# A new order for the attention and the first MLP of a fused attention and two-MLP kernel

## The chip, the cores and the metric

One core of one Trainium2 chip runs the kernel in one launch. The metric is the device time of that core in microseconds (us). Smaller is better.

## The reference

The inputs are q, k and v of shape (2, 8, 768, 64), that is two sequences with eight heads, and the weights of two MLPs. All of it is float32.

```python
# attention, per head: keys in a window of 16 to either side, and one summary key for each block of 32
k_sum = k.reshape(B, H, nb, 32, D).max(axis=3)
v_sum = v.reshape(B, H, nb, 32, D).mean(axis=3)
scores_l = where(|i - j| < 16, scale * q @ k.T, -1e9)
scores_s = scale * q @ k_sum.T + log(32)
a = softmax(concatenate([scores_l, scores_s]))
x = a @ concatenate([v, v_sum])            # (1536 tokens, 512)
# first MLP, 512 -> 2048 -> 512
h = x @ w_in;  x = (h * sigmoid(h)) @ w_out
# second MLP, 512 -> 1536 -> 512
out = ((x @ w_a) * (x @ w_b)) @ w_out2
```

## The kernel before

Every large product is made of three matmuls of parts: each float32 operand is split into a rounded high part and the rest (the low part), and high by high, high by low and low by high are added up in one PSUM bank. The weights come in as 64-bit words of which a float32 is put together on the chip.

The attention runs in 24 steps of 64 queries with all eight heads. Steps 0 to 11 belong to the first sequence. The MLPs work on blocks of 512 tokens, each of which needs eight steps, so the first MLP's work on one block stands between the attention's steps for later ones. TensorE (PE) takes its instructions in the order written, and so do VectorE (DVE), ScalarE (ACT), GpSimd (POOL) and the DMA queue on SyncE (SP).

That order, for everything up to the end of the attention, is a table of words in one string, ORDER. A loop calls one function for each word. The last letter of many words names the engine: a for ACT, v for DVE, p for POOL. The words that matter here:

- Attention step n: `sc:n` scores on PE, `sm:n` mask and row maxima on DVE, `ex:n` the exponential on ACT, `rs:n` sums and their reciprocal on DVE, `no:n` the multiplication by it, `tr:n` transposition on PE, `pc:n` copy of that out of PSUM, `av:n` the product with the values on PE, `xh:n` and `xl:n` its high and low part. `tq` and `tk` are transpositions of q and k on PE, `mk` block maxima of k on DVE.
- Value means of the first sequence: `sv:0:g` sums for head pair g on POOL or DVE, `mv:0:g` the matmuls behind them.
- Weight tile f of w_in or w_out: `da:in:f` and `du:in:f` take the two halves of the words apart (ACT, L468, and DVE, L474), `dj:in:f` joins them (DVE, L478), `hi:in:f` makes the high part (L146 on ACT, L148 on DVE), `lo:in:f` the low part (L501 on POOL or DVE). `hR` and `lR` do the last two again for a w_out tile that was put aside in DRAM.
- MLP tile i, which is block i // 16 and weight tile i % 16: `m1:i` 12 matmuls into h, `sg:i` SiLU, `gh:i` and `gl:i` high and low part of the result, `m2:i` 12 matmuls that add to y.

A softmax step has two forms. Steps in the set ACTS subtract the maximum and add up within ACT's exponential (four instructions, L393). The others subtract on POOL (`su:n`, L387), take one exponential (L396) and sum on DVE (L401).

PSUM has eight banks. Two belong to h. Four are added to the attention's two until the word `boot`, and are y's from then on. So after `boot` every `sc`, `tr`, `av`, `tq`, `tk` and `mv` takes the next of two banks in turn, here called a0 and a1, and `sc` takes both:

```python
ps = [bank(f"sc{n}")[:, 0:2 * KK].rearrange("p (a c) -> p a c", a=2) for _ in range(2)]
```

The next user of a bank waits until the one before has been read: scores by `sm`, a transposition by `pc`, an `av` by `xl`.

Of the kernel before, what the change touches and what calls it, by code (L numbers as in the profile page):

```python
# [29 lines left out]
wk:0:2:1 bq:0:1:1:v LG:0:2 sc:1 sm:1 pk:0:2:a LG:0:0 LI:1 LG:0:3 pk:0:1:v sc:0 sm:0 ex:1 sc:2 LI:0 sv:0:0:4:p LQ:0:2  # L30
sc:5 sm:2 LV:0 sm:5 ex:0 LV:1 sv:0:3:4:v rs:1 ex:2 sv:0:2:1:p mv:0:0:512:4 no:1:p ex:5 rs:0 du:in:1 mv:0:1:0:1
mv:0:2:0:1 mv:0:3:0:4 tr:1 sc:3 no:0:p rs:2 no:2:p tq:0:2:0 du:in:0 tr:0 sm:3 kv:0:0:a pc:1:a sc:4 sm:4 tq:0:2:1 su:4:p
tr:2 PV:0:1 pc:0:v rs:5 ex:3 bq:0:2:0:a sc:7 av:0 LV:2 rs:3 sm:7 ex:4 av:1 no:3:p su:7:p bq:0:2:1:a PV:0:2 LV:3 rs:4
pc:2:v da:in:1 tr:3 sc:6 no:5:p xh:0:a xh:1:a sm:6 xl:0 PV:0:3 LI:3 av:2 ex:7 tr:5 xl:1 rs:7 no:4:p pc:3:a sc:8 no:7:p
sm:8 LV:4 ex:6 LV:5 LV:6 av:3 LV:7 rs:6 xh:2:a xh:3:a no:6:p pc:5:a LI:4 tr:4 pc:4:a da:in:0 xl:2 sc:9 ex:8 dj:in:1 xl:3
sm:9 LI:2 hi:in:1:v av:5 tr:6 sc:11 lo:in:1:p av:4 xh:5:a pc:6:a tr:7 sm:11 pc:7:a rs:8 xl:5 sc:10 av:6 xh:4:a LV:8
LQ:1:0 av:7 da:in:4 m1:1:0 su:11:p ok:1 no:8:p dj:in:0 xh:6:a du:in:4 xl:4 xh:7:a xl:7 hi:in:0:a LK:1:1 lo:in:0:p xl:6
tr:8 ex:11 dj:in:4 m1:1:1 m1:0:0 ex:9 rs:11 sm:10 pc:8:a rs:9 hi:in:4:v m1:0:1 sg:1:p LO:0 da:in:3 no:9:p da:in:2
tq:1:0:0 av:8 tk:1:1:0 du:in:3 tr:9 lo:in:4:p LK:1:2 gh:1:a LI:6 du:in:2 LO:1 gl:1:p sg:0:v dj:in:2 LO:2 no:11:p
bq:1:0:0:a gh:0:a dj:in:3 du:out:0 hi:in:2:a xh:8:v tq:1:0:1 tk:1:1:1 lo:in:2:p hi:in:3:a gl:0:v da:out:0 m1:4 dj:out:0  # L40
bq:1:0:1:a sg:4:p xl:8 du:in:6 mk:1:1:0 lo:in:3:p gh:4:a du:out:1 tr:11 pc:11:a m1:2:0 pc:9:a da:in:6 da:out:1 LI:8
hi:out:0:v m1:2:1 tk:1:2:1 mk:1:2:1 dj:out:1 dj:in:6 mk:1:1:1 wk:1:1:0 LI:5 wk:1:2:1 du:in:8 SP:0 boot gl:4:p du:out:2
tk:1:2:0 hi:out:1:a hi:in:6:a sg:2:p wk:1:2:0 lo:out:0:p m1:3 da:out:2 lo:out:1:p lo:in:6:p m2:0 dj:out:2 wk:1:1:1
gh:2:a gl:2:p du:in:5 LK:1:0 da:in:5 m2:1 LO:3 SP:2 hi:out:2:v sg:3:p dj:in:5 tk:1:0:0 m1:6 LO:4 hi:in:5:a LG:1:1
mk:1:2:0 du:out:3 lo:out:2:p da:out:3 tk:1:0:1 gh:3:a LI:7 sg:6:p mk:1:0:0 mk:1:0:1 lo:in:5:p SP:1 dj:out:3 m2:2 LO:6
sk:1:v da:in:8 LO:5 hi:out:3:a du:out:4 da:out:4 SP:3 gl:3:p dj:in:8 wk:1:0:0 hi:in:8:a lo:out:3:p dj:out:4 wk:1:0:1
lo:in:8:p da:out:6 LI:10 du:out:6 pk:1:0:v LI:9 m1:5 da:in:7 du:in:7 gh:6:a m2:3 sg:5:v gl:6:p dj:out:6 dj:in:7 LV:11
du:out:5 sc:13 LO:8 hi:out:4:a hi:in:7:a gh:5:a lo:out:4:p sm:13 sc:14 gl:5:v SP:4 lo:in:7:p m1:8 hi:out:6:a da:in:9
du:in:9 m1:7 sg:8:v da:out:5 dj:in:9 sm:14 LV:9 dj:out:5 sc:12 LO:7 hi:in:9:v lo:out:6:p du:in:10 ex:10 rs:10 LG:1:2
lo:in:9:p LV:10 SP:6 m2:4 hi:out:5:a sm:12 da:in:10 lo:out:5:v sg:7:p av:9 dj:in:10 xh:9:a LI:13 no:10:p da:out:7 SP:5  # L50
ex:14 du:out:7 m2:5 m2:6 LQ:1:1 du:out:8 xl:9 LI:11 sv:1:2:1:p gh:8:a ex:13 da:out:8 hi:in:10:v dj:out:7 gh:7:a
lo:in:10:p hi:out:7:a tr:10 ex:12 gl:7:p gl:8:v SP:7 da:in:13 du:in:13 LG:1:3 sv:1:3:1:p dj:out:8 LO:9 lo:out:7:v LG:1:0
du:in:11 m1:9 LI:12 mv:1:2:256:1 sv:1:1:1:p da:in:11 dj:in:13 m1:10 pc:10:a LO:13 hi:out:8:a rs:14 du:out:9 rs:13
dj:in:11 lo:out:8:v du:in:12 av:10 sg:9:p sg:10:p mv:1:3:0:1 kv:1:2:a m2:7 SP:8 hi:in:11:a xh:10:a LI:15 hi:in:13:v
# [5 lines left out]
dj:out:11 da:in:14 PV:1:2 PV:1:3 sm:16 av:12 xh:12:a LV:14 lo:out:10:p du:in:14 gh:13:a hi:out:11:v xl:12 SP:11 m2:10  # L60
rs:15 SP:10 no:15:p da:out:13 dj:in:14 sg:12:v dj:out:13 PV:1:1 tr:13 pc:13:a sc:17 LO:15 lo:out:11:v hi:in:14:a
da:out:12 gh:12:a hi:out:13:a lo:out:13:p LO:14 lo:in:14:p sm:17 av:14 xh:14:a SP:13 gl:12:v m2:11 tr:15 xl:14 m1:15
gl:13:p da:out:15 sg:15:p du:out:12 LQ:1:2 dj:out:12 pc:15:v SP:12 du:out:14 av:15 hi:out:12:a av:13 xh:15:v da:out:14
lo:out:12:p ex:18 LV:17 m1:14 xh:13:a RO:16 xl:15 du:out:15 gh:15:v LV:16 ex:16 m2:12 hR:16:v xl:13 gl:15:p sg:14:p
dj:out:14 lR:16:v dj:out:15 m1:17 sc:19 sg:17:v ex:17 hi:out:14:a gh:17:v gl:17:v m2:13 gh:14:a sm:19 tq:1:2:0
lo:out:14:p rs:18 m1:16 hi:out:15:a tq:1:2:1 lo:out:15:v rs:17 RO:17 gl:14:p no:17:v sg:16:v bq:1:2:0:v no:18:p
bq:1:2:1:a m1:18 tr:17 m2:14 SP:15 rs:16 sg:18:v LV:18 pc:17:v sc:20 sm:20 su:19:p av:17 RO:19 first gh:16:a m2:15
gl:16:v ex:19 xh:17:v rs:19 su:20:p yh:0:1 xl:17 hR:17:a SP:14 no:19:p hR:19:v LV:21 no:16:v tr:18 m1:21 RO:18 pc:18:a
sc:22 yh:0:0 lR:17:p sm:22 yh:0:3 tr:16 yh:0:2 sg:21:p gh:18:v gl:18:v pc:16:v lR:19:v sc:21 m1:19 m2:16 gh:21:v gl:21:p
RO:20 ex:20 sg:19:p RO:23 hR:18:v sm:21 av:18 xh:18:v xl:18 m2:17 lR:18:p tr:19 ex:22 gh:19:v hR:20:a pc:19:v ex:21  # L70
av:16 gl:19:p rs:20 m1:24 m1:20 LV:19 sg:24:p m2:18 rs:22 xh:16:a rs:21 xl:16 sc:23 sg:20:v no:21:p RO:21 lR:20:v
hR:23:a sm:23 tr:21 av:19 m2:19 gh:20:a LV:20 gl:20:v LV:22 no:22:p RO:22 pc:21:a gh:24:v ex:23 m1:22 sg:22:p av:21
hR:21:a rs:23 m2:20 hR:22:a xh:19:v xl:19 gl:24:p lR:21:p RO:27 gh:22:v m1:27 LV:23 lR:23:v sg:27:p no:20:v gl:22:p
m2:21 m1:23 sg:23:p tr:22 no:23:p xh:21:v xl:21 lR:22:p tr:23 pc:23:a gh:27:v RO:25 gl:27:p hR:27:v m2:22 RO:24 pc:22:v
# [1015 lines left out]
```

## Time and profile before

| what | value |
|---|---|
| time, median of 3 runs | 640.61 us (639.71 to 643.76) |
| the profiled execution | 643.56 us, of which its span is 641.8 us |
| mean granted TensorE clock | 0.989 of full speed |
| busy: PE, DVE, ACT, POOL | 612.9, 396.1, 299.7, 303.9 us |

The span runs from the first to the last instruction. The profiled execution lies 2.95 us above the median of the runs. The attention and its share of the first MLP take the first 250 us of the span, and the words of ORDER end there.

### The profile page before, as it was taken

The page shows a single profiled execution, that of the slowest core. Times are in us where ns is not written, and L with a number is a line of the kernel's source. Part 1 is how long each engine was busy: PE and PEld are TensorE (multiplying, and loading weights), DVE is VectorE, ACT ScalarE, POOL GpSimd, SP SyncE. Part 2 cuts the span into 40 slices and gives each one's busy share as a digit, 9 for nine tenths or more (in the row PEclk, how much of TensorE's full clock was granted, in tenths as well). Part 3 has the DMA queues.
Part 4 walks back from the last instruction along what each step waited for, and adds up shares of the span by engine and source line. Part 5 has one row for each costly group of instructions (what it writes and reads, how often), then busy time and mean ns, then how long its engine had stood idle before and what let it go on. Part 6 is the DMA issues. An engine that isn't in the chain of part 4 may idle for free.

```text
span 641.8 us, 10139 instructions
## 1 busy us (share of the span) xinstructions
PE 612.9 (95%) x3632; PEld 528.8 (82%) x3632; DVE 396.1 (62%) x768; ACT 299.7 (47%) x651; POOL 303.9 (47%) x270
## 2 busy tenths in 40 slices
...
GB/s 231 204 177 258 283 249 308 154 203 103 62 46 58 59 37 146 229 221 195 165 199 189 116 49 73 191 104 225 83 213 83 229 16 97 84 182 302 142 2 132
DMA packets 90522, 97.82 MB, mean 152 GB/s; under 512 B 39000, under 2 KB 68440, under 8 KB 90472
## 3 DMA queue, kind: packets, MB, share of 16 engines
...
q8 instruction: 29, 0.48, 0.3%
q14 instruction: 21, 0.17, 0.1%
...
## 4 chain that ended last, share of the span: by engine, by line
PE 71%; DVE 4%; POOL 4%; issue 2%; ACT 0%; ACTq 0%; DVEq 0%; POOLq 0%
PE y L557 17%; PE h L524 15%; PE bankg L762 10%; PE bankh L762 10%; PE ol L808 10%; PE o L787 5%; POOL wab L645 1%; POOL ab L727 1%; PE av L428 1%; POOL w_out L501 1%; PE sc L358 1%; PE pt L414 1%; DVE yt L677 1%; DVE pts L148 0%; DVE sm L380 0%
## 5 line engine op out<-in xcount | busy, mean ns | idle before, releaser
L524 PE MATMUL h<-x,w_in 128*128 128x512 f32 (+1 forms) x612 | 143.0, 384 | 0.0
L557 PE MATMUL y<-g,w_out 128*128 128x512 f32 x576 | 141.3, 396 | 0.0
L524 PEld LDWEIGHTS h<-x,w_in 128*128 128x128 f32 x612 | 109.9, 190 | 22.3 <-issue 0.5
L557 PEld LDWEIGHTS y<-g,w_out 128*128 128x128 f32 x576 | 107.5, 189 | 23.9 <-issue 0.5
L501 POOL TENSOR_TENSOR w_out<-re_out,w_out 128x512 fp32r<-128x512 f32 x37 | 52.4, 1416 | 114.2 <-ACT w_out L146 108.0
L808 PE MATMUL ol<-w_out,plh 128*128 128x512 f32 x192 | 59.1, 389 | 0.0
L539 DVE TENSOR_TENSOR g<-h,g 128x512 fp32r<-128x512 f32 x31 | 21.4, 691 | 46.7 <-ACT g L146 46.5
L501 POOL TENSOR_TENSOR w_out<-w_out,w_out 128x512 fp32r<-128x512 f32 x23 | 32.0, 1402 | 34.1 <-ACT w_out L146 29.5
L539 POOL TENSOR_TENSOR g<-sg,g 128x512 fp32r<-128x512 f32 x17 | 24.8, 1461 | 43.7 <-DVE g L148 18.8
L727 POOL TENSOR_TENSOR ab<-sum,ab 128x384 f32<-128x384 f32 x24 | 27.9, 1171 | 32.2 <-DVE sum L724 32.1
L532 ACT ACTIVATE h<-h 128x512 f32<-128x512 f32 x31 | 18.1, 583 | 53.8 <-PE h L524 53.7
L808 PEld LDWEIGHTS ol<-w_out,plh 128*128 128x128 f32 x192 | 36.0, 188 | 7.5
L146 ACT CAST w_out<-re_out 128x512 fp32r<-128x512 f32 x38 | 23.6, 622 | 36.4 <-issue 27.5
L808 PE MATMUL ol<-w_out,pll 128*128 128x512 f32 x96 | 37.4, 389 | 0.0
L800 DVE TENSOR_TENSOR pll<-pl,plh 128x1024 fp32r<-128x1024 f32 x12 | 17.9, 1492 | 29.9 <-ACT plh L799 29.9
L787 PE MATMUL o<-w_out,p 128*128 128x512 f32 x108 | 30.7, 397 | 0.4 <-POOL w_out L501 0.2
L380 DVE CUSTOM_DVE_ANT_0 sm<-sc,mask 128x120 f32<-128x120 f32 x96 | 21.1, 276 | 15.5 <-PE sc L358 15.4
L393 ACT ACTIVATE sm<-sm,st 128x120 f32<-128x120 f32 x76 | 29.1, 390 | 1.5 <-DVE st L380 1.4
L478 DVE SCALAR_TENSOR_TENSOR w_out<-w_out,u_out 128x512 uint32<-128x512 uint32 x28 | 27.3, 974 | 3.0 <-ACT w_out L468 1.5
L762 PE MATMUL bankh<-yhT,wab 128*128 128x384 f32 x96 | 28.3, 335 | 0.7 <-DVE sum L709 0.7
L408 POOL TENSOR_TENSOR sm<-sm,st 128x480 f32<-128x480 f32 x20 | 22.6, 1136 | 11.7 <-DVE st L404 5.3
L501 POOL TENSOR_TENSOR w_in<-w_in,w_in 128x512 fp32r<-128x512 f32 x15 | 21.3, 1424 | 13.5 <-ACT w_in L146 7.9
(260 smaller groups left out, 1377.8 us busy)
## 6 DMA issues: line engine op xcount, KB each, us to landing
...
```

Of the source, the lines that this page charges most:

```text
L146: nc.scalar.copy(o, i)
L393: nc.scalar.activation(sm[:, pr, :], sm[:, pr, :], AF.Exp, scale=-1.0, bias=st[:, 0, pr:pr + 1], accum_out=st[:, 1, pr:pr + 1])
L408: engines[engine].tensor_tensor(sm, sm, st[:, 3, :, None].to_broadcast([P, NPR, KK]), op=ALU.mult)
L478: nc.vector.scalar_tensor_tensor(bits, bits, 3, u_t.pop((kind, f)), op0=ALU.logical_shift_left, op1=ALU.bitwise_or)
L501: engine.tensor_tensor(w[:, 1], w32_t[kind, f], w[:, 0].bitcast(F32), op=ALU.subtract)
L524: nc.tensor.matmul(h_ps[i][:, cols], win_t[f][:, a, c * P:(c + 1) * P], x_t[n][:, steps, m, c, :], start=(idx == 0), stop=(idx == 3 * NK - 1))
L539: engines[engine].tensor_tensor(g_t[i][:, 1], sg_t.pop(i), g_t[i][:, 0].bitcast(F32), op=ALU.subtract)
L557: nc.tensor.matmul(y_ps[n, c], wout_t[i][:, a, c * P:(c + 1) * P], g_t[i][:, m, :], start=(f == 0 and (a, m) == (0, 0)), stop=(f == N1 - 1 ...
L727: engines["v" if k == 6 else "p"].tensor_tensor(at, x, at, op=ALU.mult)
L762: nc.tensor.matmul((A, B)[b], weights(u, a, s, s + 1)[:, 0, c * P:(c + 1) * P], yc_t[q, y][m][:, c, :], start=(idx == 0 and not more), sto ...
L787: nc.tensor.matmul(o_ps[t], g[:, a, c:c + P], w[:, m], start=(begins and (a, m) == (0, 0)), stop=(ends and (a, m) == PARTS[-1]))
L808: nc.tensor.matmul(late_o[j], late_p[f][a][:, j * P:(j + 1) * P], wo2_t[N2 + f][:, m], start=(f == 0 and (a, m) == (0, 0)), stop=(f == N2 ...
```

## The change

ORDER is replaced by another order of almost the same words, and ACTS by another set. No function is changed. Steps 7, 11 and 19 join ACTS, and 10 and 23 leave it, so one subtraction fewer stands on POOL. Of the words that stay, these change their engine:

- from POOL to DVE: 11 `lo` (in 3, 4, 6, 8, 10, 11 and out 0, 2, 9, 10, 12), 9 `no` (0, 4, 8, 9, 12, 14, 18, 19, 21), 3 `lR` and 6 `gl`; from DVE to POOL: one `no`, 3 `lR`, 2 `gl` and one copy of block maxima;
- between ACT and DVE: copies and high parts (`br`, `pc`, `xh`, `hi`, `hR`, `gh`), in either direction; on balance DVE loses one `hi`, two `hR`, one `gh` and two `xh` to ACT and takes one `pc`.

```diff
-ACTS = {0, 1, 2, 3, 5, 6, 8, 9, 10, 12, 13, 14, 15, 16, 17, 18, 21, 22, 23}
+ACTS = {0, 1, 2, 3, 5, 6, 7, 8, 9, 11, 12, 13, 14, 15, 16, 17, 18, 19, 21, 22}
...
-pc:14:v m1:13 sc:18 ex:15 pk:1:2:a m2:9 du:out:10 LO:11 SP:9 no:13:v gh:11:v da:out:10 hi:in:12:a lo:in:12:p LV:13
...
+m1:12 da:out:11 pc:12:v lo:in:15:v du:out:11 sg:13:p LV:13 gh:13:a sc:16 dj:out:11 PV:1:2 hi:out:10:a da:in:14 sm:16
```

PE in the first sequence, where the value means are made (`vsum00` is the tile of the means, `vg00` to `vg03` are the four head pairs' sums, `pt1` is the transposition `tr:1`). Before:

```order
L358 MATMUL sc5_327<-kin0_169,qbm_204 64x120
L312 MATMUL vsum00_362<-vg00_283,sel_89 120x128 x4
L312 MATMUL vsum00_362<-vg01_249,sel_89 120x128
L312 MATMUL vsum00_362<-vg02_264,sel_89 120x128
L312 MATMUL vsum00_362<-vg03_287,sel_89 120x128 x4
L414 MATMUL pt1_382<-ident_87,sm1_276 120x128 x4
```

And now:

```order
L358 MATMUL sc5_326<-kin0_153,qbm_210 64x120
L312 MATMUL vsum00_358<-vg00_280,sel_89 120x128 x4
L312 MATMUL vsum00_358<-vg03_287,sel_89 120x128 x4
L312 MATMUL vsum00_358<-vg01_204,sel_89 120x128
L312 MATMUL vsum00_358<-vg02_268,sel_89 120x128
L414 MATMUL pt1_380<-ident_87,sm1_282 120x128 x4
```

The four matmuls for head pair 3, whose sums DVE makes, moved ahead of those for pairs 1 and 2, whose sums POOL makes.

DVE early in the first MLP, around the low part of the first w_out tile (`w_out0`; u tiles are `du`, w32 tiles `dj`, `ks1` is `mk`, `pts11` is `pc:11`). Before:

```order
L474 TENSOR_SCALAR u_out1_920<-st_out1_861 128x512
L148 CAST w_out0_951<-w32_out0_893 128x512
L274 TENSOR_REDUCE ks1_736<-kt121_965 128x4x8
L478 SCALAR_TENSOR_TENSOR w32_out1_946<-w32_out1_946,u_out1_920 128x512
L478 SCALAR_TENSOR_TENSOR w32_in6_944<-w32_in6_944,u_in6_914 128x512
L274 TENSOR_REDUCE ks1_736<-kt111_884 128x4x8
L474 TENSOR_SCALAR u_in8_982<-st_in8_949 128x512
L474 TENSOR_SCALAR u_out2_990<-st_out2_866 128x512
```

And now:

```order
L478 SCALAR_TENSOR_TENSOR w32_out0_908<-w32_out0_908,u_out0_871 128x512
L148 COPY pts11_928<-pt11_919 120x512
L501 TENSOR_TENSOR w_in3_905<-w32_in3_828,w_in3_905 128x512
L474 TENSOR_SCALAR u_out1_933<-st_out1_860 128x512
L274 TENSOR_REDUCE ks1_746<-kt121_954 128x4x8
L478 SCALAR_TENSOR_TENSOR w32_out1_951<-w32_out1_951,u_out1_933 128x512
L274 TENSOR_REDUCE ks1_746<-kt111_883 128x4x8
L539 TENSOR_TENSOR g4_926<-sg4_911,g4_926 128x512
L478 SCALAR_TENSOR_TENSOR w32_in6_935<-w32_in6_935,u_in6_913 128x512
L474 TENSOR_SCALAR u_in8_1007<-st_in8_917 128x512
L474 TENSOR_SCALAR u_out2_1009<-st_out2_867 128x512
L501 TENSOR_TENSOR w_out0_959<-w32_out0_908,w_out0_959 128x512
```

The low parts of `w_in3` and `w_out0` and the copy `pts11` came to DVE (the low parts from POOL), the high part of `w_out0` left it for ACT, and the low part of `w_out0` stands behind `u_out2`.

PE in the second sequence, around the transposition `pt12` (`tr:12`) and the scores `sc16`, whose two tiles are the two banks (y rows are `m2`, h rows are `m1`). Before:

```order
L414 MATMUL pt12_1719<-ident_87,sm12_1334 120x128 x4
L358 MATMUL sc16_1732<-kout1_735,qb_90 64x120
L358 MATMUL sc16_1733<-kout1_735,qb_90 64x120
...
L524 MATMUL h12_1742<-x0_522,w_in12_1703 128x512 x12
L428 MATMUL av12_1769<-pts12_1730,vw0_91 64x64 x8
L557 MATMUL y0_0_1025<-g10_1563,w_out10_1757 128x512 x3
...
L414 MATMUL pt13_1812<-ident_87,sm13_1230 120x128 x4
L358 MATMUL sc17_1819<-kin1_734,qb_90 64x120
...
L428 MATMUL av14_1850<-pts14_1649,vw2_93 64x64 x8
```

And now:

```order
L414 MATMUL pt12_1716<-ident_87,sm12_1319 120x128 x4
L524 MATMUL h12_1723<-x0_527,w_in12_1702 128x512 x12
L358 MATMUL sc16_1749<-kout1_745,qb_90 64x120
L358 MATMUL sc16_1750<-kout1_745,qb_90 64x120
...
L428 MATMUL av12_1772<-pts12_1739,vw0_91 64x64 x8
L414 MATMUL pt13_1790<-ident_87,sm13_1233 120x128 x4
L557 MATMUL y0_0_1030<-g10_1565,w_out10_1761 128x512 x3
...
L428 MATMUL av14_1832<-pts14_1644,vw2_93 64x64 x8
L414 MATMUL pt15_1850<-ident_87,sm15_1554 120x128 x4
```

The MLP tile `h12` moved between `pt12` and `sc16`, and `av12` and `pt13` now stand directly behind `sc16`. `sc17` went further down, to where it follows a whole tile of y.

## Rows read from the trace of the kernel before

**Rows 1.** Windows: stretch, length; busy us (instructions) of PE, PEld, DVE, ACT, POOL; clock, DMA, GB/s.

```profile
40.00:60.00 20.00, 19.39 (x239) 17.55 (x240) 19.76 (x52) 17.31 (x44) 14.15 (x14) 1.00 0.95 268
60.00:80.00 20.00, 20.00 (x103) 16.90 (x102) 18.41 (x25) 14.79 (x36) 13.13 (x11) 1.00 0.88 260
0.00:250.00 250.00, 226.17 (x1712) 182.45 (x1713) 159.46 (x447) 154.59 (x376) 114.22 (x112) 0.97 0.59 161
```

**Rows 2.** Timeline of PE from the value means to the first transposition.

```profile
19.64 1.35 PE L312 MATMUL vsum<-vg,sel 96*120 96x128 f32 x10 [1.48 <-POOL vg L298]
...
22.60 2.49 PE L312 MATMUL vsum<-vg,sel 96*120 96x128 f32 x10 [1.61 <-POOL vg L298]
...
24.88 1.06 PE L414 MATMUL pt<-ident,sm 128*120 128x128 f32 x4
```

**Rows 3.** Timeline of PE after `boot`: start, length, what; idle time before it and its releaser.

```profile
84.90 1.04 PE L358 MATMUL sc<-kin,qb 64*64 64x120 f32 x16 [2.05 <-DVE st L380]
...
132.02 0.63 PE L358 MATMUL sc<-kout,qb 64*64 64x120 f32 x14 [0.83 <-DVE pts L148]
...
140.28 0.63 PE L358 MATMUL sc<-kin,qb 64*64 64x120 f32 x14 [0.33 <-ACT pts L146]
141.55 0.69 PE L428 MATMUL av<-pts,vw 120*64 120x64 f32 x16 [0.64 <-PE sc L358]
...
172.16 0.69 PE L428 MATMUL av<-pts,vw 120*64 120x64 f32 x16 [0.65 <-PE sc L358]
...
180.35 0.62 PE L414 MATMUL pt<-ident,sm 128*120 128x128 f32 x4 [0.80 <-DVE st L380]
...
182.59 0.86 PE L358 MATMUL sc<-kin,qb 64*64 64x120 f32 x14 [1.27 <-DVE pts L148]
...
206.26 0.63 PE L414 MATMUL pt<-ident,sm 128*120 128x128 f32 x4 [0.69 <-DVE st L380]
```

**Rows 4.** Timeline of POOL: the low part of the first w_out tile.

```profile
62.14 1.30 POOL L501 TENSOR_TENSOR w_out<-w_out,w_out 128x512 fp32r<-128x512 f32 x1 [0.69 <-DVE w_out L148]
```

**Rows 5.** Timeline of PE at the first tiles of y.

```profile
64.84 5.61 PE L557 MATMUL y<-g,w_out 128*128 128x512 f32 x24
```

**Rows 6.** Windows around two stretches of low granted clock, columns as in Rows 1.

```profile
19.00:22.40 3.40, 1.35 (x10) 1.16 (x10) 1.79 (x13) 3.40 (x21) 3.24 (x4) 1.00 1.14 271
22.50:29.20 6.70, 6.60 (x46) 5.62 (x50) 2.54 (x15) 3.30 (x13) 3.38 (x4) 0.50 0.83 148
179.40:182.80 3.40, 1.33 (x22) 0.81 (x17) 3.06 (x12) 3.34 (x5) 0.00 (x0) 1.00 0.00 0
182.90:186.20 3.30, 3.30 (x21) 2.42 (x11) 0.23 (x1) 0.54 (x1) 0.00 (x0) 0.50 0.60 139
```

**Rows 7.** Timeline of DVE, its instructions ahead of two PE waits.

```profile
66.22 1.51 DVE L474 TENSOR_SCALAR u_out<-st_out 128x512 uint32<-128x512 uint32 x1
...
93.27 0.16 DVE L403 TENSOR_REDUCE st<-st 128x4 f32<-128x8 f32 x1 [1.21 <-ACT sm L393]
```

**Rows 8.** Timeline: POOL's first normalization.

```profile
22.66 1.26 POOL L408 TENSOR_TENSOR sm<-sm,st 128x480 f32<-128x480 f32 x1
```

**Rows 9.** Line L501, 0 to 250 us: count, ns least/median/most, first and last start.

```profile
L501 POOL TENSOR_TENSOR w_in<-w_in,w_in x15: 1265/1450/1751, 42.7 to 143.6; 128x512 fp32r<-128x512 f32 x15
...
L501 DVE TENSOR_TENSOR w_out<-w_out,w_out x5: 678/979/1361, 94.3 to 163.1; 128x512 fp32r<-128x512 f32 x5
```

**Rows 10.** Groups of DVE by line, 0 to 250 us: shapes, count, busy us, mean ns, idle before.

```profile
L478 DVE SCALAR_TENSOR_TENSOR w_in<-w_in,u_in 128x512 uint32<-128x512 uint32 x16 | 18.4, 1159 | 3.6 <-ACT w_in L468 3.4
L478 DVE SCALAR_TENSOR_TENSOR w_out<-w_out,u_out 128x512 uint32<-128x512 uint32 x16 | 15.2, 952 | 1.7 <-ACT w_out L468 1.5
L474 DVE TENSOR_SCALAR u_out<-st_out 128x512 uint32<-128x512 uint32 x16 | 14.1, 887 | 0.0
L474 DVE TENSOR_SCALAR u_in<-st_in 128x512 uint32<-128x512 uint32 x16 | 12.9, 812 | 0.0
```

**Rows 11.** The same view as in Rows 9 for line L474.

```profile
L474 DVE TENSOR_SCALAR u_in<-st_in x16: 394/800/1524, 22.7 to 133.5; 128x512 uint32<-128x512 uint32 x16
```

More of the change, by code (lines that the diff above doesn't have):

```diff
@@ L30 @@
[L30 to L54, printed above, removed]
@@ L60 @@
[L60 to L74, printed above, removed]
@@ new lines @@
+av:3 xh:2:a xh:3:a tr:4 LV:5 no:6:p pc:4:a LI:4 pc:5:v LV:7 xl:2 sc:9 ex:8 da:in:0 dj:in:1 LV:6 xl:3 sm:9 LI:2 av:5 tr:6
+hi:in:1:a sc:11 lo:in:1:p sm:11 av:4 xh:5:a tr:7 pc:6:a pc:7:a rs:8 LQ:1:0 xl:5 av:6 xh:4:a da:in:4 av:7 dj:in:0 sc:10
+xh:6:v hi:in:0:a m1:1:0 du:in:4 xh:7:v xl:7 xl:4 no:8:v lo:in:0:p ok:1 ex:11 m1:0:0 LK:1:1 rs:11 xl:6 m1:1:1 LV:8 tr:8
+ex:9 sg:1:p pc:8:a dj:in:4 hi:in:4:a tq:1:0:0 sm:10 su:10:p m1:0:1 LO:0 rs:9 da:in:3 av:8 da:in:2 tk:1:1:0 no:9:v tr:9
+du:in:3 lo:in:4:v no:11:p gh:1:a LI:6 LO:1 du:in:2 LK:1:2 LO:2 dj:in:2 bq:1:0:0:a du:out:0 tq:1:0:1 dj:in:3 sg:0:v
@@ new lines @@
+gh:0:a gl:1:p tk:1:1:1 xh:8:v m1:4 hi:in:2:a hi:in:3:a gl:0:v da:out:0 sg:4:p du:in:6 mk:1:1:0 xl:8 LI:8 tr:11 dj:out:0
+bq:1:0:1:a gh:4:a pc:11:v lo:in:3:v pc:9:a du:out:1 da:in:6 lo:in:2:p m1:2:0 da:out:1 tk:1:2:1 hi:out:0:a boot mk:1:2:1
+dj:out:1 hi:out:1:a LI:5 mk:1:1:1 wk:1:1:0 gl:4:v dj:in:6 m1:2:1 wk:1:2:1 LO:4 m1:3 du:in:8 du:out:2 tk:1:2:0 sg:2:p
+lo:out:0:v hi:in:6:a SP:0 wk:1:2:0 da:out:2 lo:out:1:p lo:in:6:v m2:0 LK:1:0 dj:out:2 gh:2:a wk:1:1:1 da:in:5 gl:2:p
+du:in:5 m2:1 LO:3 sg:3:p SP:2 hi:out:2:a lo:out:2:v dj:in:5 tk:1:0:0 hi:in:5:a m1:6 mk:1:2:0 mk:1:0:0 du:out:3 LG:1:1
```

48 lines of the change are left out of this document (39 added, 9 removed).

## The prediction

> **What bounds the kernel now.** I read the busy times first, then the windows of the stage that the order covers, then every idle gap of PE in it, and last the engines that feed PE. PE is busy for 612.9 of 641.8 us, so at most 29 us can be won. In the first 250 us it is busy for 226.2 [rows 1]: nearly all of its idle time, 23.8 us, lies where the order is changed. What follows keeps its order, and PE is idle there for 5 of 392 us, so a gain or loss before is carried to the end one for one.
>
> The 23.8 us have three parts. Until 24.9 us PE waits for loads and for the first scores. Then the value means hold it up: it waits 1.48 and 1.61 us for POOL's sums [rows 2]. After `boot`, when the attention has two banks left, PE waits for a bank that has just been filled. The reader can see in [rows 3] that every such wait ends with a reader of scores or of a transposition, and that the row ahead of it on PE is one of attention too, not an MLP tile: 2.05 us where scores follow scores, 0.83 and 0.33 where scores follow a transposition, 0.64 and 0.65 where an `av` follows scores, 0.80 and 0.69 where a transposition does, 1.27 where scores follow that transposition.
>
> Between 44 and 82 us PE has no gap. But DVE is busy for 19.76 of 20 us and then 18.41 of 20 [rows 1], and the weight tiles come just in time: the low part of the first w_out tile ends on POOL at 63.44 (62.14 + 1.30) and PE begins to use it at 64.84, 1.4 us later [rows 4, 5]. There the new order can only lose.
>
> TensorE's granted clock is at its lower level (1.2 of 2.4 GHz) in 22.5 to 29.2, after a stretch in which PE was busy for 1.35 of 3.4 us, and in 182.9 to 186.2, after one with 1.33 of 3.4 [rows 6].
>
> **The change part by part.** Durations are those of the profiled execution (643.56 us), which lies 2.95 us above the median of 640.61. I sum differences, and set them against the median.
>
> Bank waits that go. `m1:12` now stands between `tr:12` and `sc:16`, a whole tile of y lies ahead of `sc:17`, `m2:16` and `m1:19` stand around `tr:16`, and `m2:19` ahead of `tr:21`. A tile is 12 matmuls and some 2.8 us (24 in 5.61 [rows 5]), more than any wait in [rows 3]. So 0.83 + 0.33 + 0.64 + 0.80 + 1.27 + 0.69 = 4.56 us go. The 2.05 of `sc:14` behind `sc:13` and the 0.65 of `av:17` behind `sc:20` stay.
>
> Bank waits that come. `av:9` stands directly behind `sc:12`. Its bank is free after half of `sm:12`, and on DVE `sm:12` stands behind `rs:10`, which waits for ACT's exponential (1.21 us of idle time before it [rows 7]). Bounds are 0.65 and 2.05 [rows 3], and because of that exponential I take 2.0. `av:12` stands behind `sc:16`, with one join of weights ahead of `sm:16`: the same bounds, 1.0. `tr:13` and `tr:18` follow these `av` on the second bank, which is read by the time the `av` is through, or nearly: 0 to 0.80, 0.2 each. `sc:18` waits for `pc:14`, ahead of which DVE now has a sum of values and a low part: 0 to 1.27, 0.5. Sum 3.9, from 1.3 to 7.0. Net of both: -0.7 us, from -3.3 to +2.4.
>
> Value means. The eight instructions for head pair 3 (of the ten in [rows 2] that take 2.49 us from 22.60) moved to where PE waits. `tr:1` can then start when its normalization on POOL is done, 22.66 + 1.26 = 23.92 [rows 8], in place of 24.88: -1.0 us. Bounds: 0, if the sums of pair 3 are late too, and 8/10 of 2.49, -2.0.
>
> Clock, early. In 22.5 to 29.2 PE is busy all the time at half clock [rows 6], and 6.7 us of it would be 3.3 less. The same eight instructions take 1.1 us at the full clock (8/10 of 1.35) and come to lie in the thin stretch before, which would be busy for 2.4 of 3.4 us. Whether the clock then holds no row tells. Some of the gain would be lost to other waits. I take -1.5, from 0 to -3.3.
>
> Clock, late. The waits of 0.80 and 1.27 that made the stretch before 182.9 thin are gone. The 3.3 us at half clock cost 1.65. A new thin stretch can arise (`sc:16`, `av:12`, `tr:13`), so I take half: -0.8, from 0 to -1.65.
>
> Two-input work from POOL to DVE. On balance 11 `lo`, 4 `gl` and 8 `no` move. A low part takes 1.45 us on POOL and 0.68 on DVE at the least [rows 9]. But DVE's own instructions are longer when POOL runs. The joins mean 1.16 and 0.95 us [rows 10], while the shortest two-input instruction is 0.68; the shifts mean 0.81 and 0.89, the shortest is 0.39 [rows 10, 11]. Over the 250 us that is 33.6 - 32 x 0.68 = 11.8 us and 27.0 - 32 x 0.39 = 14.5 us of delay, 26 us for 114.2 us of POOL's work, 0.23 per us. The Trainium skill, SBUF — State Buffer, section Who interferes with whom, says why: a DVE instruction with two SBUF inputs and a GpSimd instruction that reads SBUF take the same port, and whoever comes second waits for all of the other. By that rule each moved low part gives DVE back the delay that it caused, and the trace agrees so far as 0.68 and 1.16 us tell.
>
> The place that decides is the first w_out tile. Its low part now stands on DVE behind `du:out:2`, which ended at 67.7 (66.22 + 1.51 [rows 7]). Ahead of it come two `no`, two `lo`, one `gl` and one `pc`, 6 x 0.67 = 4.0 us; two high parts (0.41 each) and the sum of step 11 (0.65) leave, 1.5. Without any relief the low part would end at 67.7 + 2.5 + 0.7 = 70.9, and PE, ready at 64.84, would wait 6.0 us. From 44 us on, six joins and eight shifts run there, by their means 6 x 0.38 + 8 x 0.46 = 6.0 us above their shortest. POOL has 11 instructions there before and 5 now, so half comes back, 3.0, and the wait is 3.0. In this stretch the delays are above the mean (1.51 against 0.89 for that shift [rows 7, 10]), so I take +2.0, from 0 to +6.0. Further on the slack is larger, and DVE is idle for 90 of the 250 us, so nothing more is added.
>
> The other moves between ACT and DVE are one for one at 0.4 to 0.7 us beside other work. ACT has 95 us of idle time, and the form of three steps moves 0.65 us off DVE and 1 us off POOL. I cost them at nothing. If ACT's copies came late, they would show as bank waits, within the bounds above.
>
> Sum: -0.7 - 1.0 - 1.5 - 0.8 + 2.0 = -2.0 us. That is 641.6 for the profiled execution, and 638.6 by the median.
>
> **The rivals.** First, a clear gain: the new clusters wait no longer than the 0.65 of `av:17`, DVE is relieved fully, and the clock holds. Then -3.3 - 1.0 - 2.0 (of the early clock) - 1.65 = -8.0, 632.6 us. For it: DVE's delay of 26 us is real. Against it: `sc:13` and `sc:14` stay as they are, and with DVE nearly full in 40 to 80 us a faster PE only meets the weights.
>
> Second, slower: DVE falls behind in 45 to 70 us because the low parts on it wait for ACT's high parts, with joins behind them. Price: the 6.0 us above, the bank waits at their upper end (+2.4, since `sm` stands in the same queue), no clock gain, -1.0 for the means: +7.4, 648.0 us. It decides from a relief of less than 2 us: the wait is then over 4 us and outweighs what is gained. For it: 19.76 of 20 us [rows 1] and the 1.21 us that DVE idles at a wait with reductions behind it [rows 7]. Against it: a low part takes half as long on DVE. The Trainium skill, PSUM — Partial Sum Buffer, section Engine vs sequencer instructions, speaks for this rival: it calls the queues of ScalarE, VectorE and GpSimd strictly first in, first out. By that rule nothing behind a waiting low part can pass it, and the row at 93.27 agrees.
>
> Third, nothing is won: each bank wait that goes turns up at the next attention step, and PE's idle time only moves. 640.6 us. For it: the sum has terms of both signs, the largest of 2 us.
>
> **How the numbers follow.** The forecast gets 0.48, the clear gain 0.20, slower 0.13, nothing won 0.19. The likeliest is the forecast, 638.6 us. A measurement of this kernel can tell about 1% from no change: below 634.2 is faster, above 647.0 is slower. Faster takes three quarters of the clear gain and 0.02 of the forecast's edge: 0.17. Slower takes half of the second rival and 0.01 more: 0.08. The rest, 0.75, is the same. All lower bounds together give 630.4, all upper ones 649.0; the range leaves the ends out, 631.5 to 645.5.
>
> **What would show it.** `pt` (tr:1) starting near 23.5, with the eight `vsum` matmuls before POOL's second sum, shows the third term right. A granted clock of 1.0 through 22 to 30 shows the fourth. A PE wait ahead of the first y tile, released by a low part on DVE, shows the last term, its length the size. Joins of 0.7 us in place of 1.2 between 45 and 80 us show the relief. The gaps of [rows 3] at `sc:16`, `sc:17`, `av:14`, `tr:16`, `sc:21` and `tr:21` should be gone, and new ones stand at `av:9`, `av:12` and `sc:18`. The prediction is wrong if PE shows long gaps between 45 and 82 us, or if its idle time before 25 us changes, which I left alone: the first loads are reordered there too.

## The result, and the profile after

The changed kernel takes 632.69 us (median of 4 runs, 631.82 to 633.24) against 641.11 us before (4 runs). The ratio is 0.9863, with a 95% interval from 0.9828 to 0.9898. A second set on another occasion gave 632.61 against 640.2 us, 0.9875 (0.9856 to 0.9895). So about 8 us are won, 1.3%. The forecast was 638.6 us: its direction and its range were right, its size was a quarter of what came. The time is that of the rival "a clear gain", but not by that rival's sum, as will be seen. It lies only 1.2 us inside the lower end of the range (631.5 us): that the range held is owed to its width, not to the terms of the sum.

The windows of the profile after answer to [rows 1].

```profile
core 0: us, PE busy (x) PEld busy (x) DVE busy (x) ACT busy (x) POOL busy (x), PEclk, DMA share, GB/s
40.00:60.00 20.00, 19.44 (x205) 17.99 (x204) 19.36 (x52) 18.01 (x44) 7.89 (x8) 1.00 0.94 245
60.00:80.00 20.00, 19.15 (x91) 15.56 (x90) 15.91 (x28) 14.46 (x35) 5.57 (x4) 1.00 0.90 273
0.00:250.00 250.00, 230.98 (x1765) 187.70 (x1766) 162.13 (x469) 162.26 (x396) 84.67 (x92) 0.99 0.64 170
```

PE has 4.8 us less idle time in the first 250 us (19.0 in place of 23.8). POOL lost 29.5 us of work, and DVE took over most of what POOL lost, yet is busy for only 2.7 us more; experiment 2 shows how much of that is owed to the order. The timeline of PE, after, answers to [rows 2], [rows 3] and [rows 5]: start, length, what, idle time before it and its releaser.

```profile
17.63 0.66 PE L358 MATMUL sc<-kin,qb 64*64 64x120 f32 x13 [1.10 <-DVE kin L148]
...
22.53 1.57 PE L312 MATMUL vsum<-vg,sel 96*120 96x128 f32 x12 [1.18 <-DVE vg L298]
23.95 0.65 PE L414 MATMUL pt<-ident,sm 128*120 128x128 f32 x4
...
62.14 0.71 PE L557 MATMUL y<-g,w_out 128*128 128x512 f32 x2
63.70 2.56 PE L557 MATMUL y<-g,w_out 128*128 128x512 f32 x10 [0.85 <-DVE w_out L501]
...
82.14 1.04 PE L358 MATMUL sc<-kin,qb 64*64 64x120 f32 x16 [0.76 <-DVE st L380]
...
91.96 0.69 PE L428 MATMUL av<-pts,vw 120*64 120x64 f32 x16 [2.53 <-DMA vw<-in_v_dram]
...
112.46 0.63 PE L236 MATMUL qt<-ident,raw_q 128*128 128x128 f32 x4 [0.95 <-PE sc L358]
...
131.41 0.69 PE L428 MATMUL av<-pts,vw 120*64 120x64 f32 x16 [0.65 <-PE sc L358]
132.02 0.65 PE L414 MATMUL pt<-ident,sm 128*120 128x128 f32 x4
...
169.35 0.69 PE L428 MATMUL av<-pts,vw 120*64 120x64 f32 x16 [0.65 <-PE sc L358]
...
176.71 0.60 PE L414 MATMUL pt<-ident,sm 128*120 128x128 f32 x4
177.07 2.99 PE L524 MATMUL h<-x,w_in 128*128 128x512 f32 x12
179.99 0.64 PE L358 MATMUL sc<-kin,qb 64*64 64x120 f32 x16
```

Behind 46 us PE now has six gaps, which add up to 6.4 us. Before it had twelve, together 10.6. The six waits that were forecast to go are gone: `tr:16` at 176.71 and `sc:21` at 179.99 start without a gap. Two of the five forecast to come are there, `av:9` at 91.96 and `av:12` at 131.41. `tr:13` (132.02) and the others wait for nothing.

The low part on DVE stops PE inside the first y tile for 0.85 us. `tr:1` starts at 23.95, but the first scores, at 17.63, start 2.4 us later than before (15.26). The groups of DVE, 0 to 250 us, answer to [rows 10].

```profile
L478 DVE SCALAR_TENSOR_TENSOR w_in<-w_in,u_in 128x512 uint32<-128x512 uint32 x16 | 15.4, 961 | 0.9 <-ACT w_in L468 0.8
L478 DVE SCALAR_TENSOR_TENSOR w_out<-w_out,u_out 128x512 uint32<-128x512 uint32 x16 | 11.6, 725 | 4.1 <-ACT w_out L468 3.9
L474 DVE TENSOR_SCALAR u_out<-st_out 128x512 uint32<-128x512 uint32 x16 | 9.7, 614 | 0.8 <-DMA st_out<-in_moe_w_out_dram 0.7
...
L474 DVE TENSOR_SCALAR u_in<-st_in 128x512 uint32<-128x512 uint32 x16 | 9.5, 598 | 0.1
```

Joins and shifts take 46.2 us together, 60.6 before. The windows of the clock, after, answer to [rows 6].

```profile
8.90:12.30 3.40, 2.82 (x13) 2.83 (x14) 1.22 (x2) 0.88 (x3) 0.00 (x0) 0.50 1.19 253
22.50:29.20 6.70, 6.27 (x80) 5.12 (x80) 4.64 (x27) 6.65 (x28) 2.96 (x3) 1.00 0.81 139
...
182.90:186.20 3.30, 3.30 (x30) 2.57 (x30) 1.56 (x3) 1.97 (x9) 0.00 (x0) 1.00 0.00 0
```

The clock is at its upper level at both places of [rows 6]. One stretch at half clock is left, at 8.9 us, ahead of the first scores.

Two rows of the kernel before were not counted in the forecast, and they matter below. The first is a wait whose releaser the timeline of PE calls "issue":

```profile
187.57 2.88 PE L557 MATMUL y<-g,w_out 128*128 128x512 f32 x12
191.89 0.69 PE L428 MATMUL av<-pts,vw 120*64 120x64 f32 x16 [1.44 <-issue]
```

DVE's timeline of the same stretch, before, shows what it was:

```profile
190.56 0.43 DVE L148 CAST g<-sg 128x512 fp32r<-128x512 f32 x1 [7.42 <-ACT sm L393]
190.96 0.43 DVE L148 CAST w_out<-re_out 128x512 fp32r<-128x512 f32 x1
191.30 0.28 DVE L380 CUSTOM_DVE_ANT_0 sm<-sc,mask 128x120 f32<-128x120 f32 x1
```

DVE stood idle for 7.42 us at `gh:21`, which waits for PE among others. It started 0.11 us after the y tile at 187.57 had ended (at 190.45). `sm:21` stood behind it, and `av:18` needs a bank that `sm:21` reads. The Trainium skill, PSUM — Partial Sum Buffer, section Engine vs sequencer instructions, calls such a queue strictly first in, first out; this row agrees, at a price of 1.44 us for PE. It is a wait of [rows 3]'s kind, and whoever looks only for gaps with a reader of a bank as releaser misses it.

The second is what a wait does to the step that is split by it. All score matmuls (L358) of the kernel before in 46 to 250 us, columns PE, weight loads, clock, DMA:

```profile
46.00:250.00 204.00, 9.94 (x192) 5.97 (x192) 0.98 0.53 152
```

and of the kernel after:

```profile
46.00:250.00 204.00, 8.07 (x192) 5.15 (x192) 1.00 0.56 158
```

An unbroken step of 16 takes 0.64 us (`sc:14`, directly behind `sc:13`, 1.04 before and after). `sc:16` before took 0.42 us for two matmuls, waited for 0.83, and took 0.63 us for the other fourteen [rows 3]: 0.41 us more of busy time on top of the idle time. Four steps were split so before, none after.

### The profile page after: what moved, and what is told of

Read it like the earlier page. It is cut to its first block, busy times and chain, and to the rows that moved or that the text cites. A ratio compares the mean times of both kernels' runs of the same rounds, so it can differ in the third digit from the quotient of the medians.

```text
span 630.1 us, 10119 instructions
## 1 busy us (share of the span) xinstructions
PE 605.8 (96%) x3632; PEld 524.1 (83%) x3632; DVE 392.6 (62%) x783; ACT 302.9 (48%) x663; POOL 270.4 (43%) x248
## 4 chain that ended last, share of the span: by engine, by line
PE 82%; DVE 5%; DMA 4%; POOL 4%; issue 2%; ACT 2%; SPq 1%; ACTq 0%; DVEq 0%; POOLq 0%
PE y L557 20%; PE h L524 19%; PE bankg L762 11%; PE bankh L762 10%; PE ol L808 10%; PE o L787 5%; PE av L428 2%; PE sc L358 1%; POOL wab L645 1%; PE pt L414 1%; POOL ab L727 1%; DMA st_k<-in_k_dram 1%; DMA vw<-vw 1%; DMA vw<-in_v_dram 1%; DMA sp_out<-w_out 1%
## 5 line engine op out<-in xcount | busy, mean ns | idle before, releaser
L501 POOL TENSOR_TENSOR w_out<-re_out,w_out 128x512 fp32r<-128x512 f32 x37 | 51.8, 1400 | 108.4 <-ACT w_out L146 104.3
L532 ACT ACTIVATE h<-h 128x512 f32<-128x512 f32 x31 | 18.1, 583 | 55.8 <-PE h L524 51.4
L146 ACT CAST w_out<-re_out 128x512 fp32r<-128x512 f32 x40 | 24.9, 622 | 36.5 <-issue 23.2
L539 POOL TENSOR_TENSOR g<-sg,g 128x512 fp32r<-128x512 f32 x13 | 17.9, 1379 | 44.2 <-ACT g L146 39.8
L501 POOL TENSOR_TENSOR w_out<-w_out,w_out 128x512 fp32r<-128x512 f32 x18 | 25.5, 1427 | 25.3 <-ACT w_out L146 24.3
L393 ACT ACTIVATE sm<-sm,st 128x120 f32<-128x120 f32 x80 | 30.5, 390 | 0.1
L478 DVE SCALAR_TENSOR_TENSOR w_out<-w_out,u_out 128x512 uint32<-128x512 uint32 x28 | 23.6, 844 | 5.5 <-ACT w_out L468 3.9
L705 ACT COPY sum<-bankh 128x384 f32<-128x384 f32 x12 | 5.8, 480 | 41.7 <-PE bankh L762 41.7
L645 POOL TENSOR_TENSOR wab<-c,wab 128x768 fp32r<-128x768 f32 x6 | 11.3, 1875 | 29.9 <-ACT wab L642 29.9
```

Source lines behind the costliest of these rows:

```text
L146: nc.scalar.copy(o, i)
L393: nc.scalar.activation(sm[:, pr, :], sm[:, pr, :], AF.Exp, scale=-1.0, bias=st[:, 0, pr:pr + 1], accum_out=st[:, 1, pr:pr + 1])
L478: nc.vector.scalar_tensor_tensor(bits, bits, 3, u_t.pop((kind, f)), op0=ALU.logical_shift_left, op1=ALU.bitwise_or)
L501: engine.tensor_tensor(w[:, 1], w32_t[kind, f], w[:, 0].bitcast(F32), op=ALU.subtract)
L539: engines[engine].tensor_tensor(g_t[i][:, 1], sg_t.pop(i), g_t[i][:, 0].bitcast(F32), op=ALU.subtract)
```

## The experiments

All of them change only the table of words and the set ACTS. In the first four kernels the lines stand two lower than in the listing (L499 there is L501). The kernel before ran beside each set: 641.1, 640.2 and 640.0 us in the three sets.

**1. Where the gain lies: cut at `boot`.** e1 takes the words up to `boot` from before and the rest from after; e2 the other way round. Against after, e1 is

```diff
-ok:0 LQq:0:0 br:q:0:0:v LKq:0:1 LKq:0:0 tq:0:0:1
...
-m1:2:0 da:out:1 tk:1:2:1 hi:out:0:a boot
+LQq:0:0 br:q:0:0:a LKq:0:0 LKq:0:1 tq:0:0:1
...
+LI:5 wk:1:2:1 du:in:8 SP:0 boot
```

> The words up to and with boot as before, all words behind it in the order of after. Theory A (two separate gains: the first 44 us give some 2.6 us net, the regrouped attention steps behind boot give the rest): the first w_out tile starts near 64.8 as before, without the 0.85 us wait for its low part unless DVE is behind; the bank waits of rows 3 at sc:16, sc:17, av:14, tr:16, sc:21 and tr:21 are gone; the time is 5 to 7 us below before, 634 to 636 us. Theory B (the gain hangs on DVE being relieved from the start, the regrouping only moves waits): less than 3 us below before, over 638 us.

> The words up to and with boot as after, all words behind it in the order of before. Theory A: the first MLP tile of w_in starts 2.6 us earlier than before, the bank waits of rows 3 all stand, and the time is 2 to 3 us below before, 638 to 639 us; e1 and e2 together make up the 8.4 us. Theory B: no bank wait is paid twice, so with DVE relieved early the time is nearer to after, below 636 us.

Measured: e1 636.39 us, 0.9932 (0.9916 to 0.9948); e2 639.85 us, 0.9978 (0.9958 to 0.9997). The gain does come in two parts, as theory A has it: e1 wins 4.7 us and e2 1.3, each a little less than expected (their times lie 0.4 and 0.9 us above theory A's ranges). Together that is 6.0, not all of the 8, and the intervals don't settle whether the rest is real. e1 pays 1.79 us for the low part in the first y tile, where after pays 0.85. In e2 all waits of [rows 3] stand again, the 1.44 of `av:18` as 1.42.

**2. Engines alone, order alone.** e3 gives before the engine letters of after for the low parts, normalizations and their like, where one of the two is POOL (25 net from POOL to DVE, not 28 as the expectation says); e4 takes them back in after, all but `gl:9` and `gl:19`. Some of the words, picked out of their lines:

```diff
-no:0:p no:4:p lo:in:4:p lo:out:0:p gl:3:p
+no:0:v no:4:v lo:in:4:v lo:out:0:v gl:3:v
...
```

> The order of before; only the low parts, normalizations, gate low parts and second-pass low parts go to the engine that after gives them (28 from POOL to DVE net). Theory A: the joins fall from 1.2 to about 0.7 us and DVE is no busier than before, but PE's waits are those of rows 3, so the time is within 1.5 us of before, 639.5 to 642.5 us. Theory B (relief of DVE is the gain): 3 us or more below before, under 638 us.

> The order of after, with those same instructions put back on the engine that before gives them. Theory A: the joins go back to about 1.2 us and DVE is fuller in 40 to 80 us, PE waits 0 to 3 us for weights there, and the time is within 2.5 us of after, 632 to 635 us. Theory B: the order without the relief gives less than half of the gain, over 637 us.

Measured: e3 643.14 us, 1.0033 (1.0014 to 1.0052), so 2 us slower; e4 634.88 us, 0.9901 (0.9884 to 0.9919), so 6.2 us of the gain without the engines. Both times are on the side of theory A, e3's even beyond its range. What theory A expected of DVE came in neither: the joins of e3 did not fall to 0.7 us (1.18 and 0.89 in the mean), DVE is busier, and the joins of e4 did not go back to 1.2 (0.95 and 0.85). The window of e3 and the place that decides in its PE timeline:

```profile
0.00:250.00 250.00, 228.41 (x1714) 185.15 (x1715) 167.92 (x472) 154.81 (x376) 82.88 (x87) 0.96 0.59 161
```

```profile
67.93 2.48 PE L555 MATMUL y<-g,w_out 128*128 128x512 f32 x7 [1.79 <-DVE w_out L499]
```

The relief is real but not free. Joins and shifts of e3 take 51.4 us by the same view as [rows 10], 9.2 less than before, for 31.3 us less of POOL; 8.6 of the 9.2 are the shifts'. But DVE is busy for 8.5 us more [rows 1], since the moved work is its own now. The low part of the first w_out tile came 1.79 us too late: the mechanism of the forecast's last term and of its second rival, at a third of that rival's price of 6.0. Where the 2 us of e3 are lost is not fully shown: behind 46 us PE is idle for 11.0 us, only 0.4 more than before, because `sc:14` waits for 0.69 and not 2.05; and its runs have a lower mean clock than those of the kernel before beside it (0.988 against 0.991 of full speed).

The same window and groups of e4:

```profile
0.00:250.00 250.00, 231.36 (x1755) 188.13 (x1756) 153.57 (x445) 161.07 (x395) 110.90 (x112) 0.98 0.62 168
```

```profile
L476 DVE SCALAR_TENSOR_TENSOR w_in<-w_in,u_in 128x512 uint32<-128x512 uint32 x16 | 15.2, 952 | 3.8 <-ACT w_in L466 3.8
L476 DVE SCALAR_TENSOR_TENSOR w_out<-w_out,u_out 128x512 uint32<-128x512 uint32 x16 | 13.5, 845 | 4.9 <-ACT w_out L466 4.7
L472 DVE TENSOR_SCALAR u_in<-st_in 128x512 uint32<-128x512 uint32 x16 | 12.4, 783 | 0.1
...
L472 DVE TENSOR_SCALAR u_out<-st_out 128x512 uint32<-128x512 uint32 x16 | 9.0, 573 | 0.4 <-DMA st_out<-in_moe_w_out_dram 0.4
```

POOL is nearly as busy as before, and still joins and shifts take 50.1 us, 10.5 less than before. So most of the 14.4 us that after gets back (60.6 to 46.2) comes with the order. From e4 to after, the engines give another 3.9 us for 26.2 us of POOL's time, and make DVE busy for 8.6 us more. What they may win in the new order is another thing (POOL, then PE, of e4):

```profile
56.29 2.70 POOL L499 TENSOR_TENSOR w_in<-w_in,w_in 128x512 fp32r<-128x512 f32 x2 [1.28 <-ACT w_in L144]
```

```profile
59.04 1.45 PE L522 MATMUL h<-x,w_in 128*128 128x256 f32 x10 [1.51 <-POOL w_in L499]
```

PE waits there for the second of two low parts on POOL (`lo:in:3` and `lo:in:2`). In after the first of them stands on DVE, and PE does not wait. After is 2.2 us faster than e4 by the medians, but the intervals overlap.

**3. Single pieces of the front and of `av:9`.** f0 is after itself. f1 takes the words up to `sc:1` from before. f2 and f3 move one word of after and two of before:

```diff
-lo:out:5:v SP:6 no:10:p sg:7:p av:9 m2:4 xh:9:a
+lo:out:5:v SP:6 no:10:p sg:7:p m2:4 av:9 xh:9:a
```

```diff
-LG:0:0 LI:1 LG:0:3
+LG:0:0 LG:0:3 LI:1
...
-mv:0:0:512:4 no:1:p ex:5 rs:0 du:in:1 mv:0:1:0:1 mv:0:2:0:1 mv:0:3:0:4 tr:1
+mv:0:0:512:4 no:1:p ex:5 rs:0 du:in:1 mv:0:3:0:4 mv:0:1:0:1 mv:0:2:0:1 tr:1
```

> The changed kernel itself, so that the next three can be set against it on one chip. Both theories: 631.5 to 633.5 us, 8 to 9 us below before, with one to three stretches at half clock, not always at the same places.

> The words up to and with sc:1 as before (first loads, transpositions and window copies), the rest in the order of after. Theory A (in after the first scores start 2.4 us late because the second half of k is loaded ahead of the first, and nothing gives that back): sc:1 near 15.0, tr:1 near 22 and the first w_in tile 1.5 to 2.4 us earlier than in after; 1.5 to 2.4 us below after, 630 to 631 us. Theory B (the 2.4 us is waited for again, since the value sums are bound by the transfers, whose engines are all busy until 26 us): tr:1 stays near 24, within 0.7 us of after.

> after with one word moved: the tile m2:4 of y stands ahead of av:9, as before. Theory A (the 2.53 us wait of av:9 is for a bank of sc:12, which DVE reads late, or for its values, and a tile of y covers it): the wait is gone, nothing else changes until the end of attention, 2.0 to 2.6 us below after, about 630 us. Theory B (the wait only moves: to tr:10, or to m2:5, whose low part had 2.0 us to spare): less than 1 us below after.

> before with two words moved: the load of the last group of values ahead of one weight load, and the eight matmuls of head pair 3 ahead of the sums of pairs 1 and 2. Theory A (the value-means term): tr:1 starts 0.5 to 1.0 us earlier, near 24, and the half clock in 22 to 29 us is less or gone: 1 to 2.5 us below before, 638.6 to 640 us. Theory B: tr:1 is held by the normalization on POOL and the first scores, not by the means, and the clock stretch comes as before: within 0.7 us of before.

Measured: f0 632.61 us; f1 633.3 us, 0.9875 (0.9856 to 0.9894); f2 631.84 us, 0.9859 (0.9842 to 0.9876); f3 641.53 us, 1.0016 (0.9999 to 1.0033).

f1 starts its first scores at 14.90 and still reaches `tr:1` only 0.37 us earlier than after (PE's timeline of f1):

```profile
14.90 0.76 PE L358 MATMUL sc<-kin,qb 64*64 64x120 f32 x16 [1.10 <-DVE kin L148]
...
22.64 0.48 PE L312 MATMUL vsum<-vg,sel 96*120 96x128 f32 x2 [0.24 <-POOL vg L298]
23.58 0.65 PE L414 MATMUL pt<-ident,sm 128*120 128x128 f32 x4 [0.47 <-POOL sm L408]
```

So theory B: the 2.4 us that the new order of loads costs is waited for anyway, at POOL's sums and its normalization. The first w_in tile of f1 still starts 1.5 us earlier than that of f0 (41.93 against 43.47 us), as theory A has it, but the time is not lower. Likewise f3 starts `tr:1` at 23.61 and is no faster.

In f0 the wait of `av:9` is 1.75 us and released by DVE (`sm:12`); the 2.53 us above had a late load of values on top. PE's timeline of f0:

```profile
91.27 0.69 PE L428 MATMUL av<-pts,vw 120*64 120x64 f32 x16 [1.75 <-DVE st L380]
```

f2 takes it away, and most of it comes back as a wait for a gate's low part 10 us later (PE, then DVE, of f2):

```profile
92.45 0.69 PE L428 MATMUL av<-pts,vw 120*64 120x64 f32 x16
...
103.25 3.02 PE L524 MATMUL h<-x,w_in 128*128 128x512 f32 x12 [1.03 <-DVE g L539]
```

```profile
101.20 1.40 DVE L474 TENSOR_SCALAR u_in<-st_in 128x512 uint32<-128x512 uint32 x1
102.52 0.68 DVE L539 TENSOR_TENSOR g<-h,g 128x512 fp32r<-128x512 f32 x1
```

The median is 0.8 us below f0, within both intervals.

**4. Four tiles in PE's row alone, and a combination.** k1 is before with `m1:12`, `m2:16`, `m1:19` and `m2:19` ahead of the attention step that waited (`tr:16` changes places with `yh:0:2` for that). k3 puts one low part of after back on POOL. k4 is f1, f2 and k3 together.

```diff
-sc:16 m1:12
+m1:12 sc:16
...
-tr:16 yh:0:2 sg:21:p gh:18:v gl:18:v pc:16:v lR:19:v sc:21 m1:19 m2:16
+yh:0:2 m2:16 tr:16 sg:21:p gh:18:v gl:18:v pc:16:v lR:19:v m1:19 sc:21
...
-tr:21 av:19 m2:19
+m2:19 tr:21 av:19
```

```diff
-lo:out:0:v
+lo:out:0:p
```

> before with five MLP tiles (and nothing on other engines) moved in PE's row: m1:12 ahead of sc:16, m2:16 ahead of tr:16, m1:19 ahead of sc:21, m2:19 ahead of tr:21 (for which tr:16 goes behind the y copies). Theory A (the gain lies in bank waits that a tile covers): the gaps 0.83 at sc:16, 0.80 at tr:16, 1.27 at sc:21, 0.69 at tr:21 of rows 3 and the 1.44 ahead of av:18 are gone and nothing comes for them; 4 to 6 us below before, 635 to 637 us, by far the largest part of the change with some 6 words. Theory B (each wait that goes turns up at the next attention step, for DVE's reductions set the pace): within 1.5 us of before.

> after with the low part of the first w_out tile back on POOL. Theory A (this part on DVE costs PE the 0.85 us wait inside the first y tile, the term forecast at 2.0): the wait is under 0.2 us, all later tiles up to sc:13 start 0.6 to 0.9 us earlier, and half a us or less of it is left at the end. Theory B (the wait is for the join or the high part, whoever makes the low one): the wait is 0.6 us or more.

> after with three edits: the first loads of before (words up to sc:1), m2:4 ahead of av:9, the first w_out low part on POOL. Theory A (they add up: 1.4 us at the first w_in tile, 0.9 behind the wait of av:9, 0.5 for the low part): 1.5 to 3 us below after, 630 to 631 us. Theory B (DVE, ACT and the loads set the pace between 80 and 115 us, so that PE waits there for what it gained): within 1 us of after.

Measured: k1 634.83 us, 0.9912 (0.989 to 0.9933). This is four tiles and not five, as the expectation counts, and they win 5.2 us, two thirds of the whole change and no less than all the words behind `boot` do in e1. PE's timeline of k1:

```profile
132.47 0.64 PE L358 MATMUL sc<-kout,qb 64*64 64x120 f32 x16
133.76 0.69 PE L428 MATMUL av<-pts,vw 120*64 120x64 f32 x16 [0.65 <-PE sc L358]
...
180.57 0.60 PE L414 MATMUL pt<-ident,sm 128*120 128x128 f32 x4
180.92 2.99 PE L524 MATMUL h<-x,w_in 128*128 128x512 f32 x12
183.84 0.64 PE L358 MATMUL sc<-kin,qb 64*64 64x120 f32 x16
185.13 0.69 PE L428 MATMUL av<-pts,vw 120*64 120x64 f32 x16 [0.65 <-PE sc L358]
```

The waits 0.83, 0.80, 1.27, 0.69 and 1.44 are gone. The expectation that nothing comes for them was too good: two waits of 0.65 us come, where an `av` now follows scores directly. That is the least such a pair costs in these profiles (the same 0.65 stands at `av:17` and at after's `av:12`).

k3: 631.77 us, 0.9869 (0.9846 to 0.9892). The y tile runs through (PE's timeline of k3), so the wait was for this low part on DVE:

```profile
63.38 3.00 PE L557 MATMUL y<-g,w_out 128*128 128x512 f32 x12
```

The time does not differ from after by anything that can be told. k4: 630.52 us, 0.9857 (0.9832 to 0.9883), the lowest median of all and 2.1 us below after. But set against the kernel before of its own set it is only 0.4 to 1.2 us better than after, and the intervals overlap. Its profile has a wait of 1.40 us at `m1:10`, the one that f2 shows. So it beats the kernel before; that it beats after is not shown.

## Why the prediction was right, and where its sizes failed

**Bank waits, the step that failed.** "Net of both: -0.7 us, from -3.3 to +2.4" was far too small: by the gaps of PE behind 46 us, without those for the value means and the low part, it is -4.6 us, outside the term's own range. What goes was right to the last row (4.56 us). Three things were missing beside it: the 1.44 us ahead of `av:18`, which was passed over because its releaser reads "issue"; `sc:14`, forecast to stay at 2.05, which fell to 0.76, since `sm:13` on DVE starts 0.77 us after `sc:13` (81.50 and 80.73) in place of 2.06 (84.27 and 82.21), though part of this is chance, for f3 with the words of before has 0.93; and `sc:15` with the transposition behind it (0.82 and 0.64 before, 0.95 after). A further miss is the busy time of the split steps, 1.9 us by the two rows on L358, of which the half clock at one step is a small part. What comes was forecast at 3.9 and is 2.53 + 0.65 = 3.2; in f0 it is 2.4. `av:9` alone was right in mechanism and size (2.0, measured 1.75 to 2.53). With the 0.46 us that went ahead of the second sequence's value means the idle time behind 46 us falls by 10.6 - 6.4 = 4.2 us although the low part adds 0.85. e1 and k1 show that this stage carries most of the gain.

**The weights.** The mechanism was right: PE stops in the first y tile for a low part on DVE. The size was 0.85 us in place of 2.0. In all, the relief was larger than forecast: joins at 45 to 80 us have a median of 0.68 us, and over the 250 us joins and shifts got back 14.4 us while POOL lost 29.5. But e4 shows that 10.5 of them come with the order. The engines alone gave back 9.2 us for 31.3 in the old order and 3.9 for 26.2 in the new one, 0.29 and 0.15 per us of POOL's time, on either side of the 0.23 that the forecast read. The Trainium skill, SBUF — State Buffer, section Who interferes with whom, has a DVE instruction with two SBUF inputs contend with a GpSimd instruction that reads SBUF. The trace of after agrees: the 19 joins beside which POOL runs no instruction take 0.66 to 0.69 us, the other 13 up to 1.79. So the order, too, decides which DVE instruction is delayed. The return did not cover the moved work in either order, as DVE's 8.5 and 8.6 us more show, so the second rival had a real mechanism.

**Value means and early clock.** `tr:1` came at 23.95, as forecast (23.92). No gain of that term shows all the same: f3 took 641.53 against 640.2 us, 1.0016 (0.9999 to 1.0033). Its runs also had a lower mean clock (0.9893 against 0.9926), some 0.8 us by the line given below, so a gain of that size could hide. The first loads, which the forecast left alone and named as a way to be wrong, took 2.4 us at the first scores, and f1 shows that they don't decide the time either. Idle time before 46 us fell by 0.6 us only (13.2 to 12.6). The -1.5 for the early clock was also read from one execution: the stretch at half clock sits at other places in other profiles of the same words, at 8.9 us in after and at 19.9 in f2, whose first words are the same.

**Late clock.** The profiles of all kernels bear out the direction. The forecast left out one of the three stretches of the kernel before, at 114.6 to 118.0 us, behind the waits of 0.82 and 0.64. In the thirteen profiles ten stretches at half clock lie behind 46 us, and each begins within 1.4 us of the end of a long wait of PE (the least is the pair 0.80 and 0.64). Fifteen other waits or pairs of 1.4 us and more are followed by none. The same words on PE give both: after the waits at `tr:16` and `sc:21`, f3's clock is at half,

```profile
179.30:182.70 3.40, 3.40 (x20) 2.60 (x17) 0.39 (x1) 0.70 (x1) 0.00 (x0) 0.50 0.30 92
```

and e3's is not (nor is that of e2, whose words there are those of before on every engine).

```profile
183.80:187.20 3.40, 3.40 (x27) 2.75 (x28) 0.49 (x1) 0.91 (x1) 0.00 (x0) 1.00 0.40 97
```

The old order has three or four such waits behind 46 us, the new one has one or two. The mean granted clock rises from 0.9916 (51 runs of before) to 0.9954 (10 of after), which is 5.3 and 2.9 us of lost clock. Among the runs of one kernel 1 us of lost clock goes with only 0.4 us of time (a straight line through the runs of all kernels, each about its own mean), so the clock is worth about 1 us here, where both clock terms together were put at 2.3. Why a long wait is followed by half clock in one execution and not in the next stays open.

**The sum.** -4.2 idle behind 46 us, -1.9 split steps, -0.6 in the front, some -1 by the clock: -7.7 us, against the measured -7.6 and -8.4. That these meet so closely is in part luck, for the idle time behind 46 us moves by 1.1 us between profiles of the same words: it is 10.6 in before and 9.5 in f3, 6.4 in after and 5.3 in f0. The profiles alone differ by 11.7 us, mostly since the one of before lay 2.95 above its median, with three stretches at half clock where after has one. "Other moves: nothing" was not tested by itself. That each wait turns up at the next step (the third rival) is refuted behind `boot` by k1, and borne out in front of 46 us (f1) and around 100 us (f2).
